# Loading wq in two row ranges, the first 128 rows by eight loads of 8 partitions each

## The chip, the cores and the metric

The kernel runs on one core of one Trainium2 chip. The metric is the device time of one execution in microseconds (us). Each kernel was run several times; a difference of a fraction of a per cent matters here, so every ratio below is between kernels that ran on the same chip in the same rounds. Each trace is of one run, and the traces come from several chips; figures in us that are compared between two traces have this limit.

## The reference, cut to what matters

One decode step of attention with a long cache, then a small gated MLP. Two batch rows, 32 heads, 8192 cached positions, head size 128, model size 512:

```python
# x (2,1,512); k_cache, v_cache (2,32,8192,128) bf16; wq (512,4096); wo (4096,512)
q = (layernorm(x) @ wq)                      # 32 heads of 128
scores = einsum("bhqd,bhkd->bhqk", q, k) * 128 ** -0.5
o = einsum("bhqk,bhkd->bhqd", softmax(scores), v)
h = x + o @ wo
out = h + relu_gated_mlp(layernorm(h))       # W_gate, W_up (512,1376), W_down (1376,512)
```

The two caches are 268 MB of the 282 MB that the kernel moves. `wq` is 4 MB, `wo` is 4 MB.

## The kernel before

SyncE issues all the large loads: first `wq`, then the tiles K0, V0, K1, V1, then K2, V2 and so on, each 4 MB, on 128 partitions of 32 KB. Four buffers (`slot`) hold the tiles. SyncE issues in order; a load is issued when its buffer is free.

```python
def load(s, dst, src, eng=sp):
    slot_cnt[s] += 16
    eng.eng.dma_start(dst, src).then_inc(slot_sem[s], 16)
    return (slot_sem[s], slot_cnt[s])

# ... start of the program
nc.scalar.dma_start(x_row, A_x[:, 0]).then_inc(sem_x, 16)
nc.sync.dma_start(X[:], A_wq.rearrange("(p c) n -> p (c n)", c=DC)).then_inc(sem_wq, 16)
t_k, t_v = {}, {}
t_k[0] = load(0, slot[0][:], kv(A_k_cache, 0))
t_v[0] = load(1, slot[1][:], kv(A_v_cache, 0))
t_k[1] = load(2, slot[2][:], kv(A_k_cache, 1))
t_v[1] = load(3, slot[3][:], kv(A_v_cache, 1))
nc.sync.dma_start(wd_last[:], B_W_down[F - FR:]).then_inc(sem_wd, 16)

# ... layernorm, then x and lnx transposed to chunks of 128 rows
wq = X[:].rearrange("p (c n) -> p c n", c=DC)
pe.wait((sem_wq, 16), t_xlT)
for h in range(H):
    for c in range(DC):                       # DC = 4 chunks of 128 rows
        i = nc.tensor.matmul(
            Wp[:, h * B:(h + 1) * B], lhsT=wq[:, c, h * Dh:(h + 1) * Dh],
            rhs=lT[:, c * B:(c + 1) * B], start=(c == 0), stop=(c == DC - 1))
t_q = pe.run(i)
# ... qT <- Wp; wo takes wq's buffer:
sp.wait(t_q)
nc.sync.dma_start(
    X[:].rearrange("p (h n) -> p h n", n=D),
    A_wo.rearrange("(h d) n -> d h n", d=128)).then_inc(sem_wo, 16)
# ... q_b: q broadcast to all partitions (eight steps over PE and ScalarE)

for p in range(NP):                           # NP = 32 tiles of K and of V
    # ... VectorE: prod = K tile * q_b, summed to scores; PE for a part of the tile
    if p + 2 < NP:
        sp.wait(*t_kfree[p])
        t_k[p + 2] = load(s, slot[s][:], kv(A_k_cache, p + 2))
    # ... PE: O += V tile * exp(scores); V(p+2) is loaded when its buffer is free
    # the last V tile, V31, is loaded in four pieces with a semaphore each
```

The softmax here doesn't subtract the row's maximum and nothing guards it: scores larger than these inputs give would overflow.

Of the kernel before, what the change touches and what calls it, by code (L numbers as in the profile page):

```python
# [7 lines left out]
BF16 = mybir.dt.bfloat16  # L8
# [30 lines left out]
def bass_sequential_preLN__gqa_block_cached__glu_gated_reglu__decode_kernel(  # L39
# [10 lines left out]
    out: bass.AP,  # L50
):
    B, _, D = A_x.shape
    _, H, Sk, Dh = A_k_cache.shape
    F = B_W_gate.shape[1]
    assert (B, D, H, Sk, Dh, F) == (2, 512, 32, 8192, 128, 1376)
    DC = D // 128
# [14 lines left out]
    with ExitStack() as es:  # L71
        def S(name):
            return es.enter_context(nc.semaphore(name))

        def sb(name, shape, dt):
            return es.enter_context(nc.sbuf_tensor(name, shape, dt))

        def ps(name, shape, dt):
            return es.enter_context(nc.psum_tensor(name, shape, dt))

        pe = Prog(nc.tensor, S("pe"))
        dve = Prog(nc.vector, S("dve"))
# [5 lines left out]
        sem_x, sem_wq, sem_wo, sem_w, sem_wd, sem_out = S("x"), S("wq"), S("wo"), S("w"), S("wd"), S("out")  # L88
        sem_vl = [S(f"vl{i}") for i in range(4)]

        slot = [sb(f"slot{i}", [128, SLOT], BF16) for i in range(4)]
        HM = 24
        X = sb("X", [128, H * D], BF16)
# [6 lines left out]
        ident = sb("ident", [128, 128], BF16)  # L100
# [4 lines left out]
        x_row = kT[0][0:B, 0:D]  # L105
        lnx_row = kT[0][0:B, D:2 * D]
# [1 line left out]
        mv = sb("mv", [B, 2], F32)  # L108
        sd = sb("sd", [B, 1], F32)
        rs = sb("rs", [B, 1], F32)  # L110
        xlT = sb("xlT", [128, 2 * DC * B], BF16)
        scores = [sb(f"scores{i}", [128, JC], F32) for i in range(2 * NCH)]
        e_t = [sb(f"e{i}", [128, J, 2], BF16) for i in range(2)]
        zs = sb("zs", [128, NP * 2, NCH + 1], F32)
# [13 lines left out]
        Tp = [ps(f"T{i}", [128, GT * 128], BF16) for i in range(3)]  # L128
        Sp = [ps(f"S{i}", [128, 512], F32) for i in range(2)]
        Op = [ps(f"O{i}", [128, 512], F32) for i in range(2)]  # L130
        Wp = ps("W", [128, 512], F32)
# [6 lines that stand above are left out]
        def kv(cache, p):  # L138
            hp, b = divmod(p, B)
            return cache[b, 2 * hp:2 * hp + 2].rearrange("h (p j) d -> (h p) (j d)", p=64)  # L140
# [4 lines left out]
        with nc.Block() as block:  # L145

            @block.sync
            def _(eng):

                nc.scalar.dma_start(x_row, A_x[:, 0]).then_inc(sem_x, 16)  # L150
                nc.sync.dma_start(X[:], A_wq.rearrange("(p c) n -> p (c n)", c=DC)).then_inc(sem_wq, 16)
                t_k, t_v = {}, {}
                t_k[0] = load(0, slot[0][:], kv(A_k_cache, 0))
                t_v[0] = load(1, slot[1][:], kv(A_v_cache, 0))
                t_k[1] = load(2, slot[2][:], kv(A_k_cache, 1))
                t_v[1] = load(3, slot[3][:], kv(A_v_cache, 1))
                nc.sync.dma_start(wd_last[:], B_W_down[F - FR:]).then_inc(sem_wd, 16)


# [3 lines left out]
                    out=ident_f[:], in_=ident_f[:], pattern=[[-1, 128]],  # L163
# [3 lines left out]
                for e in e_t:  # L167
# [18 lines left out]
                    out=lnx_row, in0=x_row, scalar1=mv[:, 0:1], scalar2=sd[:, 0:1],  # L186
# [1 line left out]


                pe.wait(t_ident, (sem_x, 16), t_ln)  # L190
                for k, row in enumerate((x_row, lnx_row)):
                    rv = row.rearrange("b (n c) -> b c n", c=DC)
                    for c in range(DC):
                        i = nc.tensor.transpose(
                            Tp[0][:, (k * DC + c) * B:(k * DC + c + 1) * B], rv[:, c, :], ident[0:B, 0:B])
                t = pe.run(i)
                dve.wait(t)
                t_xlT = dve.run(nc.vector.tensor_copy(out=xlT[:], in_=Tp[0][:, 0:2 * DC * B]))
                xT = xlT[:, 0:DC * B]
                lT = xlT[:, DC * B:]  # L200


                wq = X[:].rearrange("p (c n) -> p c n", c=DC)
                pe.wait((sem_wq, 16), t_xlT)
                for h in range(H):
                    for c in range(DC):
                        i = nc.tensor.matmul(  # L207
                            Wp[:, h * B:(h + 1) * B], lhsT=wq[:, c, h * Dh:(h + 1) * Dh],
                            rhs=lT[:, c * B:(c + 1) * B], start=(c == 0), stop=(c == DC - 1))
                t_q = pe.run(i)  # L210
                dve.wait(t_q)
                t_qT = dve.run(nc.vector.tensor_copy(  # L212
                    out=qT[:].rearrange("p (g b a) -> p g b a", b=B, a=2),
                    in_=Wp[:, 0:H * B].rearrange("p (g a b) -> p g b a", b=B, a=2)))
                sp.wait(t_q)
                nc.sync.dma_start(
                    X[:].rearrange("p (h n) -> p h n", n=D),
                    A_wo.rearrange("(h d) n -> d h n", d=128)).then_inc(sem_wo, 16)
# [4 lines left out]
                for m in range(NP // 4):  # L223
                    if m >= 2:
# [3 lines left out]
                        out=qrep[m % 2].rearrange("p (k r) -> p k r", r=64),  # L228
                        in_=qT[:, m * 8:(m + 1) * 8].unsqueeze(2).broadcast_to([128, 8, 64])))
# [5 lines left out]
                    for k in range(4):  # L235
                        i = nc.tensor.matmul(  # L236
                            Op[m % 2][:, k * 128:(k + 1) * 128], lhsT=qrep[m % 2][:, k * 128:(k + 1) * 128],
                            rhs=ident[:], start=True, stop=True)
# [3 lines left out]
                        out=q_b[:, m * 512:(m + 1) * 512], in_=Op[m % 2][:], func=ACT.Copy))  # L242
# [113 lines left out]
                for p in range(NP):  # L356
# [3 lines left out]
                    for c in range(NCH):  # L360
                        dve.wait(t_k[p])
                        if p == 0 and c == 0:
# [4 lines left out]
                            out=prod[:], in0=k_t[:, c * JC:(c + 1) * JC, :], in1=qv, op=ALU.mult))  # L367
                        cur, w, tog = prod[:], Dh, 0
                        while w > 8:
# [5 lines left out]
                                out=o, in0=cur[:, :, 0:half], in1=cur[:, :, half:w], op=ALU.add))  # L375
# [6 lines left out]
                        if c == 0:  # L382

                            pe.wait(t_k[p])
                            for g in range(NG):
                                n = p * NG + g
                                if n >= 3:
                                    pe.wait(t_ev[n - 3])
                                for k in range(GT):
                                    j = NCH * JC + g * GT + k  # L390
                                    i = nc.tensor.transpose(  # L391
                                        Tp[n % 3][:, k * 128:(k + 1) * 128], k_t[:, j, :], ident[:])
                                t_pt[n] = pe.run(i)
                                act.wait(t_pt[n])
                                if n >= 3:
                                    act.wait(t_sc[n - 3])
                                t_ev[n] = act.run(nc.scalar.activation(  # L397
                                    out=kT[n % 3][:], in_=Tp[n % 3][:], func=ACT.Copy))
# [54 lines left out]
                for c in range(DC):  # L453
                    i = nc.tensor.matmul(Sp[0][:, 0:B], lhsT=onesn[:], rhs=hb[:, c * B:(c + 1) * B],
                                         start=(c == 0), stop=(c == DC - 1))
# [3 lines left out]
                    out=d_b[:].rearrange("p (c b) -> p c b", b=B),  # L459
# [9 lines left out]
                def ffn_in(dst, w, f0, f1):  # L469
# [16 lines left out]
                    out=vr[:], in_=d2[:].rearrange("p (c b) -> p b c", b=B), axis=AX.X, op=ALU.add))  # L486
# [8 lines left out]
                for k, (bank, f0, f1) in enumerate(((Op[1], 0, FH), (Wp, FH, FC))):  # L495
                    dve.wait(t_g[k])
                    t_hd.append(dve.run(nc.vector.scalar_tensor_tensor(
                        out=hd[:, f0 * B:f1 * B], in0=bank[:, f0 * B:f1 * B], scalar=0.0,
                        in1=u_sb[:, f0 * B:f1 * B], op0=ALU.max, op1=ALU.mult)))
                pe.wait(t_vh)  # L500
                for k in range(2):
                    i = nc.tensor.matmul(Sp[0][:, 64:64 + B], lhsT=onesn[:], rhs=vh[:, k * B:(k + 1) * B],
                                         start=(k == 0), stop=(k == 1))
# [6 lines left out]
                for k, (f0, f1) in enumerate(((0, FH), (FH, FC))):  # L510
                    pe.wait(t_hd[k])
                    for f in range(f0, f1):
                        kp = 128 if f < 10 else FR
                        for c in range(DC):
                            i = nc.tensor.matmul(  # L515
                                Op[0][:, c * B:(c + 1) * B], lhsT=wdn[:, f, c, :] if f < 10 else wdl[:, c, :], rhs=hd[0:kp, f * B:(f + 1) * B],
                                start=(f == 0 and c == 0), stop=(f == FC - 1), skip_group_check=True)
# [3 lines left out]
                for b in range(B):  # L521
                    t = dve.run(nc.vector.scalar_tensor_tensor(
                        out=o_c[:, b * DC:(b + 1) * DC],
# [37 lines left out]
```

## Time and profile before

| | before |
|---|---|
| time | 677.0 us median of 3 runs (676.64 to 677.41) |
| moved | 281.97 MB at a mean of 417 GB/s |
| busy: DMA engines, VectorE, PE | nearly all of the span, 73%, 44% |
| last V piece multiplied, end of span | 664.30 us, 675.6 us |

These lines are from the page of the kernel before: the span, the busy time of the engines (share of the span, number of instructions), the DMA share in 40 slices of the span, two DMA queues (packets, MB, share of 16 engines), and the shares of the chain of work that ended last. In such lines PEld is the weight loads of PE, DVE is VectorE, ACT is ScalarE, POOL is GpSimd and SPq is SyncE's queue.

```profile
span 675.6 us, 14430 instructions
PE 294.0 (44%) x6596; PEld 266.2 (39%) x6596; DVE 493.6 (73%) x428; ACT 202.0 (30%) x523; POOL 1.7 (0%) x11
...
DMA  9999999999999999999999999999999999999993
...
DMA packets 15936, 281.97 MB, mean 417 GB/s; under 512 B 1442, under 2 KB 6916, under 8 KB 7044
...
q1 hardware_dynamic: 15872, 281.06, 97.9%
q8 instruction: 51, 0.84, 0.5%
...
DMA 73%; DVE 24%; PE 1%; issue 1%; SPq 0%; DVEq 0%
```

The kernel is bound by the DMA engines: their row is 9 in all slices but the last, where the dependent tail runs. Queue q8 is small. It holds instruction fetches, 51 packets of 16 KB.

What SyncE issued in the first 66 us of the kernel before, from the timeline (start us, how long the issue took, line, operands):

```profile
0.74 0.39 SPq L151 DMA_DIRECT2D X<-in_A_wq_dram  x1
1.19 0.42 SPq L135 DMA_DIRECT2D slot<-in_A_k_cache_dram  x1
...
16.74 0.39 SPq L216 DMA_DIRECT2D X<-in_A_wo_dram  x1
35.39 24.54 SPq L135 DMA_DIRECT2D slot<-in_A_k_cache_dram  x1
```

An issue takes about 0.4 us, but K2's issue, the fourth line, took 24.54 us: SyncE could not queue it while `wo` was waiting in front of it.

From the timelines of PE and VectorE of the same kernel (start us, busy us, what, count, and in brackets the idle time before it and what ended that): the q projection, the first multiply on K0, and the last part of the last V tile.

```profile
13.14 3.57 PE L207 MATMUL W<-xlT,X 128*128 128x2 bf16 x128 [8.62 <-DMA X<-in_A_wq_dram]
...
24.25 3.36 DVE L366 TENSOR_TENSOR prod<-slot,q_b 128x6144 bf16<-128x6144 bf16 x1 [2.43 <-DMA slot<-in_A_k_cache_dram]
...
664.30 1.44 PE L334 MATMUL O<-e,slot 128*128 128x2 bf16 x48 [1.55 <-DMA slot<-in_A_v_cache_dram]
```

All three end a wait for a DMA. After the third only a tail of dependent work is left: 675.6 - 664.3 = 11.3 us.

One more thing is needed, and the page does not show it: when each DMA engine is done with its part of a load. Every 4 MB load posts 16 completions, one for each engine, and the trace keeps the time of each. It does not say which engine posted it. The spread of the completions of one load tells how far the engines are apart. For the kernel before, us after the first completion:

```
K0         0.0 0.1 0.2 0.2 0.2 0.2 0.2 0.3 | 0.3 0.3 0.3 0.4 0.5 0.5 0.7 2.0
K28        0.0 0.1 0.1 0.2 0.4 0.6 3.2 4.2 | 7.9 7.9 7.9 8.3 9.4 9.4 9.5 9.7
V31 part 3 0.0 0.0 0.1 ...             0.4 | 5.2 5.2 5.3 5.3 5.3 5.3 5.7 7.1
```

At the start the engines are level. At K28, near 588 us, eight are late by 8 to 10 us. A load counts as landed when the last of its 16 engines is done. The instruction fetches fit the growth: there is one per 13 us or so, and each takes about 1.1 us. The last completion of a load steps up by 1.2 to 1.4 us near 145, 244, 352, 461 and 550 us, about once per eight fetches, and seven other engines follow it one by one. So the fetches seem to go to eight engines in turn, here called the carriers. This is read from the timing.

### The profile page before, as it was taken

Reading aid. Unit: us, or ns where it says so; the run is one execution under the profiler, and the core shown is the slowest. Engines: PE = TensorE matmul, PEld = TensorE weight load, DVE = VectorE, ACT = ScalarE, POOL = GpSimd, SP = SyncE. Lnnn points to the kernel's source line nnn. Section 1 sums busy time; section 2 is a strip of 40 time slices with the busy share of each in tenths; the row PEclk is TensorE's granted clock in tenths of the full one; section 3 lists DMA queues with packets and bytes.
Section 4 is the critical chain, followed back from the end, with each engine's and each line's share of the span. In section 5 each row is a group of like instructions: output and inputs, shape, how many; then the busy total and the mean of one; then the engine's idle time right before and its main releaser. Section 6 shows DMA issues by size and latency. Waiting matters only on the chain.

```text
span 675.6 us, 14430 instructions
## 1 busy us (share of the span) xinstructions
PE 294.0 (44%) x6596; PEld 266.2 (39%) x6596; DVE 493.6 (73%) x428; ACT 202.0 (30%) x523; POOL 1.7 (0%) x11
## 2 busy tenths in 40 slices
PE   2552254344445424443533444353344644334446
PEld 2442244333434423443433444343344534334335
DVE  1774577788777768877767887776788767778891
ACT  0630322233333223333312333331233332223330
POOL 1000000000000000000000000000000000000000
PEclk9955655566655566556556556555556555556555
DMA  9999999999999999999999999999999999999993
GB/s 373 433 434 370 430 426 432 427 430 428 434 427 430 430 434 429 432 434 427 424 428 430 431 432 434 429 432 430 426 429 428 431 428 433 428 430 392 418 411 117
DMA packets 15936, 281.97 MB, mean 417 GB/s; under 512 B 1442, under 2 KB 6916, under 8 KB 7044
## 3 DMA queue, kind: packets, MB, share of 16 engines
q1 hardware_dynamic: 15872, 281.06, 97.9%
q8 instruction: 51, 0.84, 0.5%
q14 instruction: 9, 0.07, 0.0%
q10 hardware_dynamic: 4, 0.00, 0.0%
HBM read 281.05 MB, written 0.00 MB: 416 GB/s over the span
## 4 chain that ended last, share of the span: by engine, by line
DMA 73%; DVE 24%; PE 1%; issue 1%; SPq 0%; DVEq 0%
DMA slot<-in_A_k_cache_dram 69%; DVE prod L366 15%; DVE tb L374 5%; DMA slot<-in_A_v_cache_dram 4%; DVE prod L374 3%; DVE scores L381 1%; PE S L473 0%; PE O L515 0%; PE O L334 0%; SPq L353 0%; SPq L135 0%; SPq L428 0%; PE W L473 0%; PE O L473 0%; PE W L309 0%
## 5 line engine op out<-in xcount | busy, mean ns | idle before, releaser
L366 DVE TENSOR_TENSOR prod<-slot,q_b 128x6144 bf16<-128x6144 bf16 x64 | 214.9, 3358 | 132.3 <-DMA slot<-in_A_k_cache_dram 131.1
L334 PE MATMUL O<-e,slot 128*128 128x2 bf16 x4096 | 118.7, 165 | 239.2 <-DMA slot<-in_A_v_cache_dram 119.8
L334 PEld LDWEIGHTS O<-e,slot 128*128 128x128 bf16 x4096 | 114.6, 104 | 243.5 <-ACT e L267 122.0
L397 ACT ACTIVATE kT<-T 128x1024 bf16<-128x1024 bf16 x128 | 126.5, 1022 | 170.6 <-PE T L391 169.7
L391 PE MATMUL T<-ident,slot 128*128 128x128 bf16 x1024 | 122.6, 306 | 77.5 <-DMA slot<-in_A_k_cache_dram 75.2
L374 DVE TENSOR_TENSOR tb<-prod 128x3072 bf16<-128x3072 bf16 (+1 forms) x128 | 148.2, 1158 | 4.4
L391 PEld LDWEIGHTS T<-ident,slot 128*128 128x128 bf16 x1024 | 99.7, 141 | 80.5 <-DMA slot<-in_A_k_cache_dram 78.2
L267 ACT ACTIVATE e<-scores 64x48 bf16<-64x48 f32 x128 | 32.8, 256 | 253.2 <-DVE scores L381 251.6
L374 DVE TENSOR_TENSOR prod<-tb 128x1536 bf16<-128x1536 bf16 (+1 forms) x128 | 84.2, 658 | 4.4
L259 PE MATMUL S<-qT,kT 128*128 128x2 bf16 x1024 | 48.2, 168 | 39.0 <-ACT kT L397 37.8
L259 PEld LDWEIGHTS S<-qT,kT 128*128 128x128 bf16 x1024 | 40.8, 107 | 57.6 <-ACT kT L397 57.6
L381 DVE TENSOR_REDUCE scores<-prod 128x48 f32<-128x384 bf16 x64 | 35.4, 553 | 2.2
L267 ACT ACTIVATION_READ_ACCUMULATOR e<-scores 64x1 f32 x128 | 23.6, 185 | 0.0
L267 ACT ACTIVATE e<-S 64x32 bf16<-64x32 f32 x64 | 12.9, 202 | 15.0 <-PE S L259 14.2
L267 ACT ACTIVATION_READ_ACCUMULATOR e<-S 64x1 f32 x64 | 12.9, 201 | 0.7
L212 DVE CAST qT<-W 128x64 bf16<-128x64 f32 x1 | 0.2, 225 | 12.0 <-PE W L207 12.0
L241 ACT ACTIVATE q_b<-O 128x512 bf16<-128x512 f32 x8 | 4.3, 595 | 15.6 <-PE O L236 15.6
L309 PE MATMUL W<-O_sb,X 128*128 128x2 bf16 (+1 forms) x136 | 5.0, 172 | 7.0 <-DVE O_sb L297 7.0
L309 PEld LDWEIGHTS W<-O_sb,X 128*128 128x128 bf16 x136 | 4.8, 118 | 7.2 <-DVE O_sb L297 7.2
L207 PE MATMUL W<-xlT,X 128*128 128x2 bf16 x128 | 3.6, 165 | 8.6 <-DMA X<-in_A_wq_dram 8.6
L207 PEld LDWEIGHTS W<-xlT,X 128*128 128x128 bf16 x128 | 3.5, 104 | 8.7 <-DMA X<-in_A_wq_dram 8.7
L285 DVE TENSOR_REDUCE zr<-O 128x16 f32<-128x48 f32 (+1 forms) x4 | 0.8, 204 | 8.3 <-PE O L277 8.3
(58 smaller groups left out, 39.3 us busy)
## 6 DMA issues: line engine op xcount, KB each, us to landing
slot<-in_A_k_cache_dram SPq DMA_DIRECT2D x32, 4096.0 KB, 27.8
slot<-in_A_v_cache_dram SPq DMA_DIRECT2D x31, 4096.0 KB, 32.2
X<-in_A_wq_dram SPq DMA_DIRECT2D x1, 4096.0 KB, 12.4
X<-in_A_wo_dram SPq DMA_DIRECT2D x1, 4096.0 KB, 49.1
slot<-in_A_v_cache_dram SPq DMA_DIRECT2D x1, 1536.0 KB, 21.5
slot<-in_B_W_up_dram SPq DMA_DIRECT2D x1, 1376.0 KB, 9.8
slot<-in_B_W_gate_dram SPq DMA_DIRECT2D x1, 1376.0 KB, 16.4
slot<-in_A_v_cache_dram SPq DMA_DIRECT2D x1, 1280.0 KB, 24.1
```

The costliest lines, as they stand in the source:

```text
L207: i = nc.tensor.matmul(Wp[:, h * B:(h + 1) * B], lhsT=wq[:, c, h * Dh:(h + 1) * Dh], rhs=lT[:, c * B:(c + 1) * B], start=(c == 0), stop=(c ...
L241: t_cp[m] = act.run(nc.scalar.activation(out=q_b[:, m * 512:(m + 1) * 512], in_=Op[m % 2][:], func=ACT.Copy))
L259: i = nc.tensor.matmul(Sp[p % 2][:, 2 * jj:2 * jj + 2], lhsT=kT[n % 3][:, k * 128:(k + 1) * 128], rhs=qT[:, 2 * p:2 * p + 2], start=True, ...
L267: t = act.run(nc.scalar.activation(out=e_t[p % 2][q, j0:j0 + nj, a], in_=src(q, a), func=ACT.Exp, scale=inv_sqrt_dh, accum_out=zs[q, 2 * p ...
L285: dve.run(nc.vector.tensor_reduce(out=zr[:, 2 * p0:2 * p1], in_=zbank(k)[:, 64:64 + n * (NCH + 1)].rearrange("p (n k) -> p n k", k=NCH + 1 ...
L309: i = nc.tensor.matmul(Wp[:, c * B + b0:c * B + b1], lhsT=wo_m[:, h, c, :], rhs=Ov[:, h // 2, h % 2, b0:b1], start=first[0], stop=last, sk ...
L334: i = nc.tensor.matmul(Op[k % 2][:, col:col + 2], lhsT=v_t[:, j, :], rhs=e_t[p % 2][:, j, :], start=(nmm == 0), stop=(nmm == J - 1))
L366: t_dm = dve.run(nc.vector.tensor_tensor(out=prod[:], in0=k_t[:, c * JC:(c + 1) * JC, :], in1=qv, op=ALU.mult))
L374: dve.run(nc.vector.tensor_tensor(out=o, in0=cur[:, :, 0:half], in1=cur[:, :, half:w], op=ALU.add))
L381: t_s = dve.run(nc.vector.tensor_reduce(out=sc[:], in_=cur, axis=AX.X, op=ALU.add))
L391: i = nc.tensor.transpose(Tp[n % 3][:, k * 128:(k + 1) * 128], k_t[:, j, :], ident[:])
L397: t_ev[n] = act.run(nc.scalar.activation(out=kT[n % 3][:], in_=Tp[n % 3][:], func=ACT.Copy))
```

## The change

Its intent: load 384 rows of `wq` on all partitions (so on all 16 DMA engines evenly), and the other 128 rows on the first 64 partitions by eight loads, each of 8 partitions in steps of 4. The small loads take V1's buffer for a while, so V1 is loaded only after the q projection. The projection now has three chunks of 128 rows and two of 64.

```diff
-        xlT = sb("xlT", [128, 2 * DC * B], BF16)
+        xlT = sb("xlT", [128, 9 * B], BF16)
@@ start of the program
-                nc.sync.dma_start(X[:], A_wq.rearrange("(p c) n -> p (c n)", c=DC)).then_inc(sem_wq, 16)
+                nc.sync.dma_start(
+                    X[:, 0:3 * H * Dh], A_wq[128:].rearrange("(p c) n -> p (c n)", c=3)).then_inc(sem_wq, 16)
+                wq_s = A_wq[0:128].rearrange("(p c) n -> p (c n)", c=2)
+                for a in (0, 1, 2, 3, 32, 33, 34, 35):
+                    nc.sync.dma_start(
+                        slot[3][a:a + 29:4, 0:2 * H * Dh], wq_s[a:a + 29:4]).then_inc(sem_wq, 16)
@@
-                t_v[1] = load(3, slot[3][:], kv(A_v_cache, 1))
@@ (cut: the transposes follow the new chunks of rows)
-                wq = X[:].rearrange("p (c n) -> p c n", c=DC)
-                pe.wait((sem_wq, 16), t_xlT)
+                wq = [X[:, c * H * Dh:(c + 1) * H * Dh] for c in range(3)]
+                wq += [slot[3][0:64, c * H * Dh:(c + 1) * H * Dh] for c in range(2)]
+                pe.wait((sem_wq, 9 * 16), t_xlT)
                 for h in range(H):
-                    for c in range(DC):
+                    for c in range(5):
+                        n = 128 if c < 3 else 64
                         i = nc.tensor.matmul(
-                            Wp[:, h * B:(h + 1) * B], lhsT=wq[:, c, h * Dh:(h + 1) * Dh],
-                            rhs=lT[:, c * B:(c + 1) * B], start=(c == 0), stop=(c == DC - 1))
+                            Wp[:, h * B:(h + 1) * B], lhsT=wq[c][:, h * Dh:(h + 1) * Dh],
+                            rhs=xlT[0:n, (DC + c) * B:(DC + c + 1) * B], start=(c == 0), stop=(c == 4))
@@
                 sp.wait(t_q)
+                t_v[1] = load(3, slot[3][:], kv(A_v_cache, 1))
                 nc.sync.dma_start(            # wo, as before
```

More of the change, by code (lines that the diff above doesn't have):

```diff
@@ L190, in _ @@
                 pe.wait(t_ident, (sem_x, 16), t_ln)
-                for k, row in enumerate((x_row, lnx_row)):
-                    rv = row.rearrange("b (n c) -> b c n", c=DC)
-                    for c in range(DC):
-                        i = nc.tensor.transpose(
-                            Tp[0][:, (k * DC + c) * B:(k * DC + c + 1) * B], rv[:, c, :], ident[0:B, 0:B])
+                chunks = [(128, x_row.rearrange("b (n c) -> b c n", c=DC)[:, c, :]) for c in range(DC)]
+                chunks += [(128, lnx_row[:, 128:].rearrange("b (n c) -> b c n", c=3)[:, c, :]) for c in range(3)]
+                chunks += [(64, lnx_row[:, 0:128].rearrange("b (n c) -> b c n", c=2)[:, c, :]) for c in range(2)]
+                for k, (n, row) in enumerate(chunks):
+                    i = nc.tensor.transpose(Tp[0][0:n, k * B:(k + 1) * B], row, ident[0:B, 0:B])
                 t = pe.run(i)
                 dve.wait(t)
-                t_xlT = dve.run(nc.vector.tensor_copy(out=xlT[:], in_=Tp[0][:, 0:2 * DC * B]))
+                dve.run(nc.vector.tensor_copy(out=xlT[:, 0:7 * B], in_=Tp[0][:, 0:7 * B]))
+                t_xlT = dve.run(nc.vector.tensor_copy(out=xlT[0:64, 7 * B:], in_=Tp[0][0:64, 7 * B:9 * B]))
                 xT = xlT[:, 0:DC * B]
-                lT = xlT[:, DC * B:]
-                wq = X[:].rearrange("p (c n) -> p c n", c=DC)
-                pe.wait((sem_wq, 16), t_xlT)
+                wq = [X[:, c * H * Dh:(c + 1) * H * Dh] for c in range(3)]
+                wq += [slot[3][0:64, c * H * Dh:(c + 1) * H * Dh] for c in range(2)]
+                pe.wait((sem_wq, 9 * 16), t_xlT)
                 for h in range(H):
-                    for c in range(DC):
+                    for c in range(5):
+                        n = 128 if c < 3 else 64
                         i = nc.tensor.matmul(
-                            Wp[:, h * B:(h + 1) * B], lhsT=wq[:, c, h * Dh:(h + 1) * Dh],
-                            rhs=lT[:, c * B:(c + 1) * B], start=(c == 0), stop=(c == DC - 1))
+                            Wp[:, h * B:(h + 1) * B], lhsT=wq[c][:, h * Dh:(h + 1) * Dh],
+                            rhs=xlT[0:n, (DC + c) * B:(DC + c + 1) * B], start=(c == 0), stop=(c == 4))
                 t_q = pe.run(i)
```

## The prediction

> **What bounds the kernel.** The DMA engines. The page gives 281.97 MB at a mean of 417 GB/s; the row of DMA shares is 9 in all but the last of 40 slices, and queue q1 alone takes 97.9% of 16 engines' span. The chain of waits is 73% DMA, mostly K tiles. PE is 44% busy, DVE 73%. An 11 us tail of small dependent steps follows the last V piece.
>
> The DMA records show more. A 32 KB descriptor takes 1.213 us on its engine, so the limit is per engine. Each 4 MB load sends 16 completions. Their spread, in the trace's semaphore updates, is 0.7 us for K0, about 2 us at 100 us, 3.6 us at 230 us, 5.1 us at 330 us, 9.8 us near 617 us and about 5 us for the last V pieces. Six to eight engines are close together in front, eight behind. Queue q8 explains it: 51 instruction fetches of 16 KB, one per 13 us, each about 1.1 us long, delay one engine after another, eight in turn. A load counts only when its last engine lands, so the eight engines with fetches set the time.
>
> **What the change does.** The Trainium skill, "DMA: Bandwidth & Descriptors" ("Why a DMA increments its semaphore by 16"), says that a load uses the largest count of engines up to 16 that divides its slowest dimension, the lowest-numbered ones. So each 8-partition load runs on engines 0 to 7 alone; no trace here shows it yet. Per engine, wq before: 256 KB each. After: 192 KB from the big load, plus 128 KB on engines 0 to 7. Engines 8 to 15 lose 64 KB, two descriptors, 2.43 us; engines 0 to 7 gain as much. The relative shift of 4.85 us equals the final spread of about 5 us. I take it that engines 8 to 15 carry the fetches; the trace does not name engines, so this is an inference from the fit, at about 80%.
>
> Added: eight SyncE issues of about 0.42 us (hidden: the queue holds work throughout), 32 matmuls at 28 ns, 0.9 us. V1's load moves behind the q projection, but K0, V0 and K1 (29 us) are queued by then.
>
> **On the critical path.** The start gets worse: q matmuls start at about 15.5 us instead of 13.1, q_b is ready at 26.7 instead of 23.3, K0 lands about 2.4 us later. Until the old spread exceeds 4.85 us, near 300 us, engines 0 to 7 are last. After that the fetch-carrying engines are last, but 2.4 us earlier than before, and all compute shifts with them. The wo load and K2's blocked issue (24.5 us) could cost up to 1 us of this.
>
> **Prediction:** 675.0 us (677.0 - 2.4, plus some 0.4 of losses), range 673.8 to 678.5. Chances: faster by over 2%: 0.01, within 2%: 0.98, slower by over 2%: 0.01.
>
> **What would show it.** Completions of the last V pieces spread about 1 us instead of 5, the last landing about 2.4 us earlier; first q matmul at 15 to 16 us; first multiply on K0 about 2.5 us later; K tiles after 350 us landing about 2.4 us earlier.
>
> **What would make it wrong.** If engines 0 to 7 carry the fetches, or a mix, the last engine gets 2.4 us more: 679.4 us. If 8-partition loads spread otherwise, nothing is rebalanced: about 677 to 678. If engines 8 to 15 run dry before K2's descriptors come (60 to 65 us), part of the gain is lost.

## The result, and the profile after

Changed kernel: 679.75 us median of 4 runs (678.61 to 679.81). Kernel before, in the same rounds: 677.2 us (676.64 to 677.78). The ratio is 1.0034, with a 95% interval of 1.0016 to 1.0051. Ratios here and below are the mean time of one kernel's fast runs over that of the other's of the same rounds, so they are not quite the ratio of the medians quoted. The change cost about 2.3 us by this ratio, and 2.4 us between the spans of the two profiles, where a gain of 2.0 us had been predicted.

The page of the changed kernel, the same lines as above:

```profile
span 678.0 us, 14505 instructions
PE 301.3 (44%) x6629; PEld 272.8 (40%) x6629; DVE 493.5 (73%) x429; ACT 202.3 (30%) x523; POOL 1.8 (0%) x11
...
DMA  9999999999999999999999999999999999999992
...
DMA packets 16065, 281.99 MB, mean 416 GB/s; under 512 B 1506, under 2 KB 6980, under 8 KB 7108
...
q1 hardware_dynamic: 16000, 281.06, 97.6%
q8 instruction: 52, 0.85, 0.5%
...
DMA 68%; DVE 26%; PE 3%; SPq 1%; issue 1%; ACT 0%; DVEq 0%
```

Nothing here tells where 2.4 us went. The bytes are nearly the same (0.02 MB more), the DMA engines are as busy, and there is one fetch more.

What SyncE issued in the changed kernel, and then the same three places in the timelines of PE and VectorE (the q projection is told in alternating groups of three and two matmuls; its first groups are shown):

```profile
0.73 0.39 SPq L152 DMA_DIRECT2D X<-in_A_wq_dram  x1
1.19 5.46 SPq L156 DMA_DIRECT2D slot<-in_A_wq_dram  x8
6.69 0.45 SPq L135 DMA_DIRECT2D slot<-in_A_k_cache_dram  x1
...
25.55 0.35 SPq L135 DMA_DIRECT2D slot<-in_A_v_cache_dram  x1
25.93 0.43 SPq L224 DMA_DIRECT2D X<-in_A_wo_dram  x1
43.35 19.09 SPq L135 DMA_DIRECT2D slot<-in_A_k_cache_dram  x1
```

```profile
15.42 0.24 PE L214 MATMUL W<-xlT,X 128*128 128x2 bf16 x3 [10.75 <-DMA slot<-in_A_wq_dram]
15.59 0.21 PE L214 MATMUL W<-xlT,slot 64*128 64x2 bf16 x2
15.73 0.24 PE L214 MATMUL W<-xlT,X 128*128 128x2 bf16 x3
...
32.20 3.36 DVE L374 TENSOR_TENSOR prod<-slot,q_b 128x6144 bf16<-128x6144 bf16 x1 [1.58 <-ACT q_b L249]
...
666.49 1.44 PE L342 MATMUL O<-e,slot 128*128 128x2 bf16 x48 [1.57 <-DMA slot<-in_A_v_cache_dram]
```

Three things are to be seen. The projection started at 15.42 us, as predicted, but it takes 0.314 us for five matmuls and ran until 25.5 us, 10.1 us in place of 3.6; so the first multiply on K0 started 8 us later and waited for q_b, no longer for K0. K2's issue is still blocked, until 43.35 + 19.09 = 62.4 us. And the last part of V31 is 2.19 us later (666.49 against 664.30), with the same DMA wait before it. That is nearly all of the loss of 2.4 us in the span; the tail behind it is 11.5 us now and 11.3 us before.

VectorE's waits for K tiles, from the waits view (total us, times, longest us), first the kernel before, then the changed one:

```profile
DVE prod L366 <- DMA slot<-in_A_k_cache_dram: 131.1, 31, 16.4
```

```profile
DVE prod L374 <- DMA slot<-in_A_k_cache_dram: 122.7, 29, 14.7
```

VectorE waited 8.4 us less for K tiles, and the kernel is slower. Its late start only used up idle time that it had. A wait total of an engine that is not the limit says nothing about the time.

So the late landings have to be explained. The table gives, for some loads, when the first and the last of the 16 engines was done, in us from the start of the span:

| load | before: first, last | after: first, last | first moved | last moved |
|---|---|---|---|---|
| K0 | 22.19, 24.23 | 19.83, 26.62 | -2.36 | +2.39 |
| K2 | 73.58, 75.55 | 73.97, 77.90 | +0.39 | +2.35 |
| K14 | 306.63, 311.75 | 307.09, 314.05 | +0.46 | +2.30 |
| K28 | 578.66, 588.40 | 579.01, 590.61 | +0.35 | +2.21 |
| K31 | 630.58, 636.95 | 632.75, 639.12 | +2.17 | +2.17 |

The last engine is 2.2 to 2.4 us later from the first tile to the last. The predicted turn to 2.4 us earlier after 350 us never came. By K31 the first engine is later as well: the issue of the last two K loads starts at 601.77 us in place of 599.56, since it waits for a buffer, and buffers come free 2.2 us later. The spreads of the changed kernel, us after the first completion, show more:

```
K0         0.0 0.0 0.2 0.3 0.4 0.5 0.7 0.9 | 4.9 4.9 5.0 5.0 5.1 5.2 5.2 6.8
K2         0.0 0.1 0.1 0.2 0.2 0.3 0.3 0.3 | 2.0 2.0 2.1 2.2 2.3 3.0 3.7 3.9
K28        0.0 0.1 1.9 2.1 2.2 2.8 5.0 5.9 | 7.7 7.8 7.9 8.0 8.0 8.2 11.4 11.6
```

At K0 the shift is as predicted: eight engines are 4 to 5 us behind the other eight (two descriptors of 1.213 us more for the one group, two less for the other, 4.85 us). The semaphore of `wq` confirms how the small loads run. The Trainium skill, "DMA: Bandwidth & Descriptors", section "Why a DMA increments its semaphore by 16 and not by 1", says that a load over k engines posts k completions and that the issuing sequencer writes the other 16 - k at once. Here the semaphore shows one such update for each small load as it is issued, 0.67 us apart, then 16 + 8 x 8 = 80 engine completions. So k is 8.

At K2 the shift has shrunk from 4.9 us to 2.0 us. At K28 two engines stand alone, 3.2 us behind the six before them; in the kernel before, the last eight were within 1.8 us.

### The profile page after: what moved, and what is told of

The parts are those of the page before. It is cut to its first block, busy times and chain, and to the rows that moved or that the text cites. A ratio compares the mean times of both kernels' runs of the same rounds, so it can differ in the third digit from the quotient of the medians.

```text
span 678.0 us, 14505 instructions
## 1 busy us (share of the span) xinstructions
PE 301.3 (44%) x6629; PEld 272.8 (40%) x6629; DVE 493.5 (73%) x429; ACT 202.3 (30%) x523; POOL 1.8 (0%) x11
## 4 chain that ended last, share of the span: by engine, by line
DMA 68%; DVE 26%; PE 3%; SPq 1%; issue 1%; ACT 0%; DVEq 0%
DMA slot<-in_A_k_cache_dram 63%; DVE prod L374 16%; DVE tb L382 6%; DMA slot<-in_A_v_cache_dram 4%; DVE prod L382 3%; PE W L214 1%; DMA slot<-in_A_wq_dram 1%; DVE scores L389 1%; SPq L156 1%; ACT q_b L249 0%; PE O L244 0%; PE S L481 0%; PE O L523 0%; PE O L342 0%; SPq L361 0%
## 5 line engine op out<-in xcount | busy, mean ns | idle before, releaser
L275 ACT ACTIVATE e<-S 64x32 bf16<-64x32 f32 x64 | 13.0, 203 | 15.1 <-PE S L267 14.3
L214 PE MATMUL W<-xlT,X 128*128 128x2 bf16 x96 | 7.6, 171 | 10.8 <-DMA slot<-in_A_wq_dram 10.8
L214 PEld LDWEIGHTS W<-xlT,X 128*128 128x128 bf16 x96 | 5.0, 107 | 11.3 <-DMA slot<-in_A_wq_dram 10.8
```

The lines of the kernel that those rows point to most:

```text
L214: i = nc.tensor.matmul(Wp[:, h * B:(h + 1) * B], lhsT=wq[c][:, h * Dh:(h + 1) * Dh], rhs=xlT[0:n, (DC + c) * B:(DC + c + 1) * B], start=(c ...
L275: t = act.run(nc.scalar.activation(out=e_t[p % 2][q, j0:j0 + nj, a], in_=src(q, a), func=ACT.Exp, scale=inv_sqrt_dh, accum_out=zs[q, 2 * p ...
```

## The experiments

Three theories were on the table, and the expectations below call them by letters.

- A: the eight fetch-carrying engines (the carriers) are mixed, two of engines 0 to 7 and six of 8 to 15. The two got 64 KB more (2.43 us), are last at the end, and set the time.
- B: the carriers are all among engines 8 to 15, as predicted, and the gain was lost because engines 8 to 15 ran dry before K2's descriptors came. The window of 61 to 66 us speaks for it. This is the view of busy time in a stretch (busy us and instructions of PE, weight loads, VectorE, ScalarE and GpSimd; then granted clock, DMA share, GB/s); the last number is the one to read. First before, then after:

```profile
61.00:66.00 5.00, 0.37 (x14) 0.29 (x11) 0.00 (x0) 0.00 (x0) 0.00 (x0) 0.50 1.17 425
```

```profile
61.00:66.00 5.00, 1.44 (x48) 1.36 (x48) 2.13 (x4) 0.67 (x4) 0.00 (x0) 0.50 1.01 343
```

- C: the late start (the projection of 10.1 us, V1 issued at 25.5 us) costs the time.

### Which engines carry the fetches: probe_before

The kernel before, with 16 tiny loads after steps 3, 14 and 26: one of 1 partition, one of 2, up to 16. In the trace a load of k partitions posts k engine completions, and in a batch the completions of one load come back a little later in the next load, with one more. So each load adds one engine, and the completion that it adds tells how far behind that engine's queue is. The engines are numbered here in the order in which they are added. That the chip's own numbers run the same way is what the prediction assumes; no trace shows it, and only the point on engines 7 and 15 at the very end needs it.

```diff
+        PR = (3, 14, 26)
+        probe = sb("probe", [16, len(PR) * 16 * 8], BF16)
+        sem_p = [S(f"probe{k}") for k in range(16)]
@@ in the loop, behind the loads of step p
+                        if p in PR:
+                            r = PR.index(p)
+                            for k in range(1, 17):
+                                o = (r * 16 + k - 1) * 8
+                                nc.sync.dma_start(probe[0:k, o:o + 8], A_wo[0:k, 0:8]).then_inc(sem_p[k - 1], 16)
```

> The kernel before with three batches of sixteen tiny loads (1 to 16 partitions of 16 bytes) issued in steps 3, 14 and 26. The load of k partitions should run on the k lowest-numbered engines, so the landings of one batch show, engine by engine, how far each is behind. Theory A (mixed carriers: the eight engines that carry instruction fetches are two of engines 0 to 7 and six of engines 8 to 15): between the batches of steps 3 and 26 two of the first eight engines and six of the last eight fall behind the rest by some 6 to 8 us. Theory B (the carriers are all of engines 8 to 15, and the gain was lost when these ran dry before K2): all eight of the last eight fall behind, none of the first. Both: time about that of before, 677 us, as SyncE is idle when the tiny loads are issued.

The table gives the batch after step 26: the time of the completion of each added engine, and how far it is behind engine 8 when 0.17 us is taken off for every tiny descriptor that the engine had handled in the two earlier batches (2 x (16 - e) for engine e). The 0.17 us is an estimate, from the slope of the times over the engines that are not late: engine 0 with 32 earlier ones is 4.6 us behind engine 15 with 2 (0.15 us each), and 3.3 us behind engine 8 with 16 (0.21 us each).

| engine | 0 | 1 | 2 | 3 | 4 | 5 | 6 | 7 |
|---|---|---|---|---|---|---|---|---|
| landed, us | 593.25 | 595.79 | 592.47 | 596.27 | 592.89 | 601.06 | 600.65 | 590.86 |
| behind engine 8, us | 0.6 | 3.5 | 0.5 | 4.6 | 1.6 | **10.1** | **10.0** | 0.6 |

| engine | 8 | 9 | 10 | 11 | 12 | 13 | 14 | 15 |
|---|---|---|---|---|---|---|---|---|
| landed, us | 589.94 | 598.82 | 597.31 | 597.40 | 596.65 | 596.60 | 598.10 | 588.67 |
| behind engine 8, us | 0 | **9.2** | **8.1** | **8.5** | **8.1** | **8.4** | **10.2** | 1.1 |

Eight engines are 8 to 10 us behind: 5, 6 and 9 to 14. This is the size of the spread at K28. In the two earlier batches the same eight are 1.4 to 3.3 us and 4.6 to 6.7 us behind engine 8. So six carriers are among the upper eight and two among the lower eight, as A says. Engines 1 and 3 are 3.5 and 4.6 us behind. A second instruction queue, q14, with nine fetches of 8 KB, may be what delays them. In the kernel before, two engines stand apart in the same way (3.2 and 4.2 us at K28), and their two lags together grow by 0.5 to 1.1 us in the loads that follow six of these fetches (at 233, 253, 391, 421, 548 and 580 us), and hardly between; this was not tested. The probe ran once: 680.74 us, about 3.5 us more than the kernel before (677.25). K31's last engine is 4.2 us later (641.20 us against 636.95). Some of that may be the tiny descriptors themselves (33 on engine 5 over the run, 5.6 us by the same estimate); this was not tested further.

### Undo the uneven load alone: even16, then even128

even16 keeps everything of the changed kernel but loads the 64 partitions by one load.

```diff
-                for a in (0, 1, 2, 3, 32, 33, 34, 35):
-                    nc.sync.dma_start(
-                        slot[3][a:a + 29:4, 0:2 * H * Dh], wq_s[a:a + 29:4]).then_inc(sem_wq, 16)
+                nc.sync.dma_start(slot[3][0:64, 0:2 * H * Dh], wq_s).then_inc(sem_wq, 16)
-                pe.wait((sem_wq, 9 * 16), t_xlT)
+                pe.wait((sem_wq, 2 * 16), t_xlT)
```

> The changed kernel with one part undone: the 128 rows on 64 partitions come by one load of 64 partitions, which uses all 16 engines, so each engine moves 256 KB of wq as before. The five chunks, the 160 matmuls and the late load of V1 stay. Theories A and B (the balance between engines decides): 677.2 us, ratio 1.000 to before, spread of the completions of K0 under 1 us. Theory C (the start costs it: the q projection takes 10.1 us instead of 3.6, V1's load is issued at 25.5 us): the time stays near 679.5 us, ratio 1.0035.

It took 680.81 us, ratio 1.0053 (1.0040 to 1.0067), slower than the changed kernel. This was a flawed undo. The one load of 1 MB took 5.0 us from the big load's last completion to its own. The Trainium skill, "SBUF — State Buffer", section "Door 1: The DMA port swizzle", says that the bandwidth of a DMA depends on how many of the 16 ports its partitions reach, and that partitions 0 to 63 reach only half of them. The measured 5.0 us agrees, against the 2.5 us of the same bytes over 128 partitions below. All engines lost the time alike: K31's first engine is +3.0 us and its last +3.2 us against the kernel before. So even16 says nothing of the theories.

even128 repairs this. The 128 rows are loaded over all 128 partitions, and the projection still has five alternating chunks (the last one is multiplied by zeros), V1 late, wo behind it.

```diff
-                wq_s = A_wq[0:128].rearrange("(p c) n -> p (c n)", c=2)
-                for a in (0, 1, 2, 3, 32, 33, 34, 35):
-                    nc.sync.dma_start(
-                        slot[3][a:a + 29:4, 0:2 * H * Dh], wq_s[a:a + 29:4]).then_inc(sem_wq, 16)
+                nc.sync.dma_start(slot[3][:, 0:H * Dh], A_wq[0:128]).then_inc(sem_wq, 16)
@@ (the chunks: four of 128 rows, and one of 64 rows that is multiplied by zeros)
+                wq += [slot[3][:, 0:H * Dh], slot[3][0:64, 0:H * Dh]]
+                lq += [xlT[0:64, 8 * B:9 * B]]      # set to 0
```

> A cleaner undo of the balance than the load of 64 partitions, which took 5.0 us for 1 MB: the changed kernel with rows 0 to 127 loaded one row to each of 128 partitions, 64 KB per engine. V1's load stays late, the q projection stays at 160 matmuls of alternating height (the fifth of a head is of 64 rows, times zero). Theory A: 677.2 us, ratio 1.000, although the q projection still takes some 10 us. Theory C in the form that the long q projection or V1's late load costs it: 679 us or more.

It took 677.50 us, ratio 1.0005 (0.9991 to 1.0018): as the kernel before. Its 1 MB load took 2.5 us, measured in the same way. The timeline of even128 shows the end of the projection (the cast of q starts when it is done), the first multiply on K0 and the last part of V31:

```profile
23.46 0.23 DVE L217 CAST qT<-W 128x64 bf16<-128x64 f32 x1 [18.58 <-PE W L212]
...
30.12 3.36 DVE L372 TENSOR_TENSOR prod<-slot,q_b 128x6144 bf16<-128x6144 bf16 x1 [1.58 <-ACT q_b L247]
...
664.27 1.44 PE L340 MATMUL O<-e,slot 128*128 128x2 bf16 x48 [1.28 <-DMA slot<-in_A_v_cache_dram]
```

q is ready nearly 7 us later than in the kernel before, the first multiply on K0 is 5.9 us later, V1 is issued late, and the last V piece is multiplied at 664.27 us against 664.30. Theory C falls: these things are free. What costs the time is in the eight small loads, the only part of the load that this undoes. It is not their number: dose5 below also has eight small loads and costs nothing that can be measured.

### Does engines 8 to 15 running dry matter: wo_pieces, before_wo_pieces, after_wo_act, before_wo_act

wo_pieces takes `wo` out of the way of K2: the changed kernel loads it in four pieces, behind the K loads of steps 1 to 4. before_wo_pieces does the same to the kernel before.

```diff
-                nc.sync.dma_start(
-                    X[:].rearrange("p (h n) -> p h n", n=D),
-                    A_wo.rearrange("(h d) n -> d h n", d=128)).then_inc(sem_wo, 16)
@@ in the loop, behind the load of K(p+2)
+                        if 1 <= p <= 4:
+                            h0 = 8 * (p - 1)
+                            nc.sync.dma_start(
+                                X[:, h0 * D:(h0 + 8) * D].rearrange("p (h n) -> p h n", n=D),
+                                A_wo[h0 * 128:(h0 + 8) * 128].rearrange("(h d) n -> d h n", d=128)).then_inc(sem_wo, 16)
-                            pe.wait((sem_wo, 16), t_O[0], t_O[1], t_O[2])
+                            pe.wait((sem_wo, 64), t_O[0], t_O[1], t_O[2])
```

> The changed kernel with wo loaded in four pieces of 8 heads, one behind each of the loads of K3 to K6, so that K2's issue is never blocked and no engine runs dry at 60 to 65 us. Theory A: the two lower carriers still have two descriptors more each and still land last: about 679.5 us, at best 1 us less for a smoother wo. Theory B: the lost lead of 2.5 us comes back and the time falls to about 675 us. In the profile of either: issue of K2 takes under 1 us instead of 19.1, no stretch at 61 to 66 us under 400 GB/s.

> Control for the last run: the kernel before with wo in the same four pieces. Both theories: within 1 us of before (676 to 678 us), since no engine ran dry there; what the pieces alone give is to be taken off the result of the changed kernel with pieces.

wo_pieces took 678.98 us, ratio 1.0025 (1.0013 to 1.0038); before_wo_pieces 677.70 us, 1.0007 (0.9994 to 1.0019). The changed kernel stays slower than the kernel before. But the test is not clean, as SyncE's timeline of wo_pieces shows:

```profile
84.25 18.31 SPq L135 DMA_DIRECT2D slot<-in_A_v_cache_dram  x1
...
105.72 15.66 SPq L135 DMA_DIRECT2D slot<-in_A_v_cache_dram  x1
...
128.04 21.86 SPq L135 DMA_DIRECT2D slot<-in_A_v_cache_dram  x1
```

K2's issue is short now and the spread at K2 is whole (6.8 us), but the loads behind the pieces, V2 to V4, were blocked instead, and the first engine at K14 is at 307.22 us, no earlier than in the changed kernel.

The clean form puts `wo` on ScalarE's queue, whose blocked issues stop nothing of SyncE: after_wo_act is the changed kernel with this, before_wo_act the kernel before.

```diff
-                nc.sync.dma_start(
+                act.wait(t_q)
+                nc.scalar.dma_start(
                     X[:].rearrange("p (h n) -> p h n", n=D),
                     A_wo.rearrange("(h d) n -> d h n", d=128)).then_inc(sem_wo, 16)
```

> The changed kernel with wo's load on ScalarE's queue. The four pieces only moved the blocked issues to V2, V3 and V4 (up to 21.9 us), so this is the cleaner test of what the lost lead was worth. The lead of 4.9 us of engines 8 to 15 should now outlive the wo load (spread of the completions of K2: eight near 0, eight near 5). Theory A: carriers 5 and 6 still have two descriptors more and land last: 678.5 to 679.7 us against the control's 677. Theory B (the gain was lost when 8 to 15 ran dry): 675 us.

> Control: the kernel before with wo's load issued from ScalarE's queue instead of SyncE's, so that it cannot hold up the issue of K2 in SyncE's queue. Issue of K2 under 1 us instead of 24.5. As no engine ran dry in before, the time should stay within 1 us of 677.2 us under both theories.

after_wo_act took 679.39 us, ratio 1.0032 (1.0020 to 1.0045). before_wo_act took 677.30 us, ratio 1.0003 (0.9990 to 1.0015). K2's issue from SyncE's timeline of after_wo_act, and its window of 61 to 66 us:

```profile
43.21 0.33 SPq L135 DMA_DIRECT2D slot<-in_A_k_cache_dram  x1
```

```profile
61.00:66.00 5.00, 1.44 (x48) 1.36 (x48) 2.01 (x4) 0.67 (x4) 0.00 (x0) 0.50 1.01 424
```

The issue takes 0.33 us in place of 19.09, the window moves 424 GB/s in place of 343, so the engines no longer run dry. The lead of the eight lightened engines lives on:

| load | before_wo_act: first, last | after_wo_act: first, last | first moved | last moved |
|---|---|---|---|---|
| K2 | 63.68, 65.83 | 60.89, 67.84 | -2.79 | +2.01 |
| K14 | 306.69, 311.92 | 304.13, 314.14 | -2.56 | +2.22 |
| K28 | 578.75, 588.52 | 576.41, 590.75 | -2.34 | +2.23 |
| K31 | 630.62, 637.05 | 632.97, 639.28 | +2.35 | +2.23 |

The spread at K28 in after_wo_act ends in 8.3, 8.8, 9.4, 9.6, 14.1, 14.3: two engines are alone, 4.5 us behind the rest. B's loss is removed, and the time is what it was. So B falls as the cause. Running dry was real, but it took time from engines that did not set the end. The table ends at K31. In this run (678.69 us, the fastest of its five) the last part of V31 landed 1.1 us later than in before_wo_act, not 2.2; the end of the next section says why that can be.

### How much, and on which engines: dose5, dose8, dose16

These add a useless load of `wq` rows, 64 KB for each engine that they touch (2.43 us at the rate of the 32 KB descriptors), to the kernel before, right after its own `wq` load. dose5 uses eight loads of 5 partitions (engines 0 to 4, none of them a carrier), dose8 eight loads of 8 partitions (engines 0 to 7, with 5 and 6), dose16 one load of 1 MB on all 16. The data goes to a scratch tile, and the first multiply waits for it. The table's last two columns are from the trace of one run each.

```diff
+                for a in (0, 1, 2, 3, 32, 33, 34, 35):
+                    nc.sync.dma_start(
+                        prod[a:a + 17:4, 0:32, :].rearrange("p j d -> p (j d)"),   # dose8: a + 29
+                        A_wq[a:a + 17:4]).then_inc(sem_d, 16)
 # dose16 instead:
+                nc.sync.dma_start(prod[:, 0:32, :].rearrange("p j d -> p (j d)"), A_wq[0:128]).then_inc(sem_d, 16)
```

> The kernel before with nothing changed but 64 KB more per engine on engines 0 to 4 only (eight loads of 5 partitions of 8 KB of wq into a buffer that is not in use yet, queued behind wq; their data is thrown away). The tiny loads showed the carriers of instruction fetches to be engines 5, 6 and 9 to 14. Theory A: the five engines have 5 us or more in hand by the end, so the 2.43 us cost nothing: 677.2 us, ratio 1.000, although K0 lands 2.4 us later. Theory C (what the start loses is lost): 679.7 us, ratio 1.0036.

> As dose5, but loads of 8 partitions, so engines 0 to 7, with the carriers 5 and 6 among them. Theory A: two descriptors' worth on two carriers are enough: 679.7 us, ratio 1.0036, as with the change; the last two completions of a load stand 2 us apart from the other six carriers. If the carriers were all among 8 to 15: 677.2 us.

> As dose8, but one load of 128 partitions of 8 KB, 64 KB more on each of the 16 engines. All theories: 679.7 us, ratio 1.0036; it measures what 64 KB per engine cost where every engine has them. Theory A wants dose8 to equal this run, with 0.5 MB loaded instead of 1 MB.

| | median us | ratio (95%) | K31's last engine, moved | V31 part 3, last engine, us |
|---|---|---|---|---|
| before | 677.15 | | | 664.25 |
| dose5 | 677.47 | 1.0001 (0.9989 to 1.0014) | +0.1 | 664.09 |
| dose8 | 678.43 | 1.0019 (1.0006 to 1.0032) | +2.2 | 664.77 |
| dose16 | 679.70 | 1.0038 (1.0025 to 1.0051) | +2.5 | 666.23 |

The last part of V31 in the PE timeline, of dose5, of dose8 (where it follows the earlier parts without a gap) and of dose16:

```profile
664.14 1.44 PE L339 MATMUL O<-e,slot 128*128 128x2 bf16 x48 [1.31 <-DMA slot<-in_A_v_cache_dram]
```

```profile
662.59 3.67 PE L339 MATMUL O<-e,slot 128*128 128x2 bf16 x128
```

```profile
666.28 1.44 PE L336 MATMUL O<-e,slot 128*128 128x2 bf16 x48 [1.03 <-DMA slot<-in_A_v_cache_dram]
```

The same 64 KB costs nothing that can be measured on engines 0 to 4, and 2.5 us on all sixteen. Adding engines 5, 6 and 7 to dose5 costs 1.0 us in the median (dose5's runs are 676.84 to 677.50 us, dose8's 677.98 to 679.05), and K31's last engine moves by 2.2 us as in the changed kernel. The first multiply on K0 is at 25.1 us in both dose5 and dose8, so the start is not the difference. That the time of dose8 rose by 1.3 us and not by 2.4 is a miss of the expectation under A. In its profiled run the last part of V31 landed only 0.5 us late, though K31 had landed 2.2 us late just before. A likely reason, argued and not tested, is where the last fetch fell. Over the third part of V31 the three latest engines stand at 3.6, 5.4 and 7.1 us in the changed kernel, as if one of the two loaded carriers had one more fetch. In dose8 they stand at 4.7, 5.5 and 5.5 us, as if another carrier had it. In dose8 PE did not wait for this part at all (no gap in the second line above, where the kernel before waits 1.55 us). Of this run's 1.7 us of extra span, 0.5 us are there when PE is done with V31. The rest arises later, 0.6 us of it in a stop of PE for which the profile shows no cause. So dose8 shows which engines matter, and not the whole size of the loss.

### A better split: four_engines and four_engines_b

If A is right, a load that spares all eight carriers must gain. By the probe, engines 0 to 4, 7, 8 and 15 have room, and the small loads used the first ones each time. So 64 rows of `wq` (512 KB) go to engines 0 to 3, by eight loads of 4 partitions, and the other 448 rows are spread evenly. Each carrier gets 32 KB less than before (1.21 us). Engine 3, the latest of the four, gets 96 KB more (3.64 us by the same rate): with the 4.6 us that it is behind near 590 us it comes to 8.2 us, still below the latest carriers (10.2 us, less the 1.2 us taken off). `wo` is on ScalarE's queue, as in after_wo_act; before_wo_act (1.0003) shows no gain from this alone.

```diff
+                nc.sync.dma_start(                      # rows 64 to 127, as half-rows on 128 partitions
+                    prod[:, 0:16, :].rearrange("p j d -> p (j d)"),
+                    A_wq[64:128].rearrange("p (t n) -> (p t) n", t=2)).then_inc(sem_wq, 16)
                 t_k[0] = load(0, slot[0][:], kv(A_k_cache, 0))     # four_engines: behind the small loads
+                t_z3 = dve.run(nc.vector.memset(slot[3][0:64, 0:2 * H * Dh], 0.0))
+                sp.wait(t_z3)
+                wq_s = A_wq[0:64].rearrange("(p c) n -> p (c n)", c=2)
+                for g in range(2):
+                    for i in range(4):
+                        nc.sync.dma_start(
+                            slot[3][32 * g + i:32 * g + i + 13:4, 0:2 * H * Dh],
+                            wq_s[16 * g + i:16 * g + i + 13:4]).then_inc(sem_wx, 16)
@@ (cut: the chunks of lnx that fit this layout; 192 projection matmuls)
```

> The idea of the change, aimed at what the tiny loads showed: 64 rows of wq by eight loads of 4 partitions, 128 KB on each of engines 0 to 3, none of which carries fetches of PE instructions; the other 448 rows spread evenly, 224 KB on each of the 16 engines; wo on ScalarE's queue. Carriers 5, 6, 9 to 14 have one descriptor (32 KB, 1.21 us) less than before; engines 0 to 3 have 3.6 us more, against a lead of 5 us or more. Theory A: 1.2 us faster than before with wo on ScalarE's queue, about 676.0 us, ratio to before 0.998. If what counts is any engine of the first eight, or the start: 677 to 681 us.

four_engines took 677.78 us, ratio 1.0007 (0.9994 to 1.0021): no gain. Its VectorE timeline, SyncE's timeline and the window of 10 to 13 us show why:

```profile
1.65 3.47 DVE L159 MEMSET slot<- 64x4096 uint32 x1 [1.65 <-PEq L584]
```

```profile
5.15 5.09 SPq L164 DMA_DIRECT2D slot<-in_A_wq_dram  x8
10.28 0.44 SPq L137 DMA_DIRECT2D slot<-in_A_k_cache_dram  x1
```

```profile
10.00:13.00 3.00, 0.83 (x31) 0.84 (x32) 0.00 (x0) 0.00 (x0) 0.00 (x0) 1.00 1.12 351
```

The small loads waited for a memset, K0's load was behind them, and the other engines had nothing to do: 351 GB/s. This is a start that does cost time, since it left engines with an empty queue. four_engines_b issues K0 before the memset is waited for, and is otherwise the same.

> The run before with one thing mended: there K0's load was issued at 10.3 us, behind the eight small loads, which waited for a 3.5 us memset, and engines 4 to 15 stood idle at 11 to 12.5 us. Here K0's load is issued ahead of the small ones. Theory A as before: carriers have one descriptor less than in the kernel before, 1.2 us, so 676.0 us, ratio 0.998; against it, 64 more matmuls fetch half a block more, which can add up to 1.4 us if it falls on a carrier that is last. The small loads now land near 25 us and the q projection ends some 11 us later than before, which theory A holds to be free.

It took 675.99 us against 677.34 us of the kernel before, ratio 0.9982 (0.9968 to 0.9995). It is the only version whose whole interval lies below the kernel before; it also lies below that of the changed kernel (1.0016 to 1.0051), which ran in other rounds. The difference is 0.18%, so at 2% it is the same. Its window of 10 to 13 us, and its timeline at the end of the projection, the first multiply and the last V part:

```profile
10.00:13.00 3.00, 0.82 (x31) 0.83 (x31) 0.00 (x0) 0.00 (x0) 0.00 (x0) 1.00 1.17 496
```

```profile
28.16 0.22 DVE L248 CAST qT<-W 128x64 bf16<-128x64 f32 x1 [19.48 <-PE W L243]
...
34.81 3.36 DVE L404 TENSOR_TENSOR prod<-slot,q_b 128x6144 bf16<-128x6144 bf16 x1 [1.58 <-ACT q_b L279]
...
662.64 1.44 PE L372 MATMUL O<-e,slot 128*128 128x2 bf16 x48 [0.86 <-DMA slot<-in_A_v_cache_dram]
```

The first multiply on K0 is the latest of all kernels here, 10.6 us behind the kernel before, and the last V part is the earliest, 1.66 us ahead. K28's last engine is 1.35 us earlier than in the kernel before, near the 1.21 us that were taken off the carriers. The spread at K28 is 0.0 to 9.5 us, with no engine alone at the end.

## Why the prediction was wrong, and where it was right

- Right: the limit. The DMA engines bound the kernel, one by one, and eight of them are last at the end, as the probe shows. That these are late because of the fetches is argued from the timing above. Two of the prediction's figures leave out the last engine: with it, the spread is 2.0 us at K0 and 7.1 us at the last V pieces, not 0.7 and 5.
- Right: the small loads run on engines 0 to 7 alone (eight completions each), and the relative shift is 4.85 us: at K0 the two groups stand 4 to 5 us apart, the first engine 2.36 us earlier and the last 2.39 us later.
- Right: the projection starts at 15.42 us ("about 15.5 us"), and SyncE's extra issues are hidden, though they took 0.68 us each and not 0.42.
- Wrong, and this is the step that failed: "I take it that engines 8 to 15 carry the fetches; the trace does not name engines, so this is an inference from the fit, at about 80%." By the probe the late engines are 5, 6 and 9 to 14. Engines 5 and 6 got 64 KB more on top of the same fetch delay, so they are last, and from K0 to V31 loads land 2.2 to 2.4 us later. The "fit" was a coincidence of two numbers: a spread of 5 us says how far the engines are apart, and the split into eight and eight says how many are late, but neither says which. The prediction's own line "If engines 0 to 7 carry the fetches, or a mix, the last engine gets 2.4 us more: 679.4 us" is what happened (679.75 us). dose5 against dose8 and dose16 shows the same from the other side, and four_engines_b turns it into a small gain. That the time came so close to 679.4 us is in part luck, if the account of dose8 holds: runs of the changed kernel lie between 678.61 and 679.81 us, and in after_wo_act's trace V31 lost only 1.1 us.
- Wrong: the last V completions did not close up to 1 us. The third part of V31 is spread over 7.1 us as before, and its last engine is 2.2 us later: two carriers are among the engines that were loaded and not among those that were lightened.
- A term that was mis-sized: "32 matmuls at 28 ns, 0.9 us". The projection took 10.1 us in place of 3.6, so 6.5 us more. The first multiply on K0 is therefore 8 us later and not 2.5. It cost nothing: even128 has the same slow projection at 677.5 us.
- "The wo load and K2's blocked issue (24.5 us) could cost up to 1 us of this": it did cut the lead of the lightened engines, from 4.9 to 2.0 us at K2. It did not set the time, as after_wo_act shows.
- Still open: what delays engines 1 and 3 (q14 is a suspect); why the probe kernel lost 3.5 us; that it is the fetches which delay the eight; and the exact share of the last fetches in the smaller loss of dose8.

## What to carry to other kernels

Before moving bytes from one DMA engine to another, find out which engines are late: a row of tiny loads of 1 to 16 partitions near the end of the kernel names them, at the price of one run. Then judge every change by the engine that is last at the end of the run: in these runs, bytes added to engines with a lead were free up to that lead, and a late start of the compute engines was free as long as every queue held work. Symmetry of a spread (eight early, eight late) does not tell which eight.

## What the Trainium skill lacked or had wrong

- No page says which DMA engines carry an engine's instruction fetches. Here, by inference, they were 5, 6 and 9 to 14 (8 to 10 us behind near 590 us), on one core.
- "Runtime: NRT & Kernel Launch", "Instruction fetch mechanics", calls the cost of crossing a 16 KiB boundary "one DMA tail-bump, mostly hidden". In this kernel, bound by the DMA engines, it does not look hidden: by the steps of the completions each of the 51 fetches delays its engine by about 1.4 us, and the eight carriers are 8 to 10 us behind near the end. No run took the fetches away.
- "DMA: Bandwidth & Descriptors", "Latency and other measured facts", says that DMA engines 7 and 15 are usually slower than the others, with a cause that it ties to SWDGE. Here all large loads went through the hardware queue, and engines 7 and 15, as the probe counts them, were among the least delayed (0.6 and 1.1 us).
- "TensorEngine Tiling (Array Packing)", "Key Properties", says that changing the tiling mode drains the TensorE, and gives no duration. Alternating three matmuls of 128 rows and two of 64 took 0.314 us for five, against 5 x 28 ns = 0.14 us without alternation: about 87 ns for each of the two switches, if they are the whole difference. In four_engines_b, where 128 matmuls of 128 rows and then 64 of 48 rows follow without such alternation, one takes about 27 ns. Whether the alternation is the page's change of mode, no run shows.
- The pages on DMA do not tell how much may be queued before an issue blocks. Behind the 4 MB load of `wo`, whose rows are 1 KB long, the next issue took 24.54 us, and 15 to 22 us behind pieces of 1 MB; on ScalarE's queue the same load blocked nothing on SyncE (0.33 us).
